# Small extra loads of wo rows from ScalarE and GpSimd in a decode kernel fed by one stream of large loads

## Chip, cores and metric

The kernel runs on one core of one Trainium2 chip. The metric is the device time of one execution in microseconds, taken as the median of several runs. Of the kernel before, three runs are shown: 694.17, 694.26 and 695.5 us, median 694.26 us. A further execution was profiled; its records are what the views below show.

## The reference

One token passes through two blocks whose results are mixed by a gate. Cut to what matters:

```python
q = (x @ wq)                                # 32 heads of 128, x is 1x512
k, v = k_cache, v_cache                     # 8 KV heads x 32768 x 128, each serves 4 query heads
p = softmax(q . k * 128**-0.5)              # over the 32768 keys
a = (p . v) @ wo                            # wo is 4096 x 512
b = (silu(x @ w1) * (x @ w3)) @ w2          # 512 -> 1792 -> 512
g = sigmoid(sum(x * gate_w))
out = g * a + (1 - g) * b
```

Everything is float32. The two caches are 134 MB each, so nearly all the bytes that the kernel reads are keys and values, each of them used once.

## The kernel before

All large loads are issued by SyncE (SP) on one queue, in the order in which the program lists them. A large load brings 128 partitions of up to 64 KB, 8 MB in all, into one of two buffers, `big_a` and `big_b`. First comes wq, then 16 key units (two heads, a quarter of the keys each), w1 and w3 after the fourth key unit, and 16 value units. From the fifth key unit on, keys and values alternate: keys into `big_a`, values into `big_b`. At the end stand four value units with the two halves of wo between them, and then w2 in five pieces of falling size (`parts`, four, four, three, two and one of its 14 row groups), whose last one ends the stream of loads.

The loop over key units, `for t in range(NH)`, has 16 rounds. In each round ScalarE copies three quarters of the second half of the unit away (`set_aside`, L318), VectorE transposes the unit in eight steps (`scores`, L346), TensorE multiplies each transposed piece with the queries (L330), ScalarE copies the scores out (L358), and TensorE works on the value unit of four rounds before (L432). After every fourth round there is a softmax (L379 to L398), and `own` reduces the value result of a head pair into one of six tiles `red` (L448). After the loop, `heads`, `place` and `mix` turn the six tiles into rows, multiply them with the first half of wo, and the last two head pairs follow as their values come in. The last matmuls (L676) use the last pieces of w2, VectorE copies the sum out (L688), and SyncE and ScalarE store two rows of 512 B each (L485).

The order is written out by hand. `Program.add` records every operation with the tiles that it reads and writes and works out which semaphores it must wait for; an operation waits for the last writer of what it reads or writes and for the readers of what it overwrites. Each engine then issues its own operations strictly in order, so an operation that waits holds up everything behind it on the same engine. The scores and values of the loop run from a loop on TensorE (L703 to L735).

GpSimd sets constants at the start (L213 to L223) and then does nothing until the end, where it waits for the two stores (`wait_ge(pr.semaphore("stored"), 32)`). ScalarE issues two small loads at the start (x and gate_w, L202, one row of 2 KB each) and one of the two stores at the end.

Of the kernel before, what the change touches and what calls it, by code (L numbers as in the profile page):

```python
# [13 lines left out]
P = 128  # L14
# [102 lines left out]
def kernel(  # L117
# [13 lines left out]
    nc = tc.nc  # L131
# [23 lines left out]
    pr = Program(nc, tc.alloc_semaphore)  # L155
    pe, dve, act, pool = (
        lambda fn, _e=e, **kw: pr.add(_e, fn, **kw) for e in ("PE", "DVE", "ACT", "POOL")
    )
    V, A, T = nc.vector, nc.scalar, nc.tensor

    def sbuf(name, *shape):
        return nc.alloc_sbuf_tensor(name, [P, *shape], F32)[:]
# [13 lines left out]
    rows = [probs[:, 0, 512 * i:512 * i + 512] for i in range(2)]  # L176
    tmp = sbuf("tmp", 2, 4, P)
    silu, prod = (tmp[:, i].rearrange("p b d -> p (b d)") for i in range(2))
    red = [sbuf(f"red{h}", P) for h in range(6)]
    acc = sbuf("acc", 512)  # L180
    otp = sbuf("otp", 16, 32)
    htp = sbuf("htp", FR, 32)
# [7 lines left out]
    def load(dst, src, writes, over=()):  # L190
        lanes[0] += 1
        lane = f"load{lanes[0] % 9}"
        return pr.add(
            "SP", lambda: nc.sync.dma_start(dst, src), writes=writes, over=[*over, lane], inc=lane, by=16, also=lane,  # L194
        )
# [13 lines left out]
    gate, sums, recip, on = sbuf("gate", 2), sbuf("sums", 32), sbuf("recip", 32), sbuf("on", 32)  # L209
    mt, mtt, mark, mark2 = sbuf("mt", 32), sbuf("mtt", 32), sbuf("mark", 1), sbuf("mark2", 1)  # L210
    quads, high, wide_t, top = sbuf("quads", 4), sbuf("high", 1), sbuf("wide_t", 32), sbuf("top", 32)
    G = nc.gpsimd
# [12 lines left out]
    for src, dst, view, axes in (  # L225
# [11 lines left out]
            reads=[src], writes=[dst])  # L237
# [6 lines left out]
    def clear(**kw):  # L244
        pe(zeros,
           reads=["acc"], writes=["s"], **kw)
# [15 lines left out]
    for c in range(NC):  # L262
# [19 lines left out]
        reads=["gate0"], writes=["gate1"])  # L282
# [4 lines left out]
    for b in range(2):  # L287
        qt = kt[b][:, 0:512]
        dve(lambda b=b, qt=qt: V.transpose(qt, rows[b]), reads=[f"row{b}"], writes=[f"kt{b}"])
        for j in range(4):  # L290
            w, u = divmod(4 * b + j, 2)
            src = qt[32 * j:32 * j + 32, :].rearrange("p (q c x) -> p x c q", q=4, c=4)[:, 0]
            for e in range(2):
                r, o = 2 * u + e, 16 + 8 * e + 4 * u
                dst = win[32 * r:32 * r + 32, w, :, o:o + 4]
# [8 lines left out]
    def where(t):  # L304
        return 1 if t in (0, 2) else 0

    def load_keys(t):
        b = where(t)
        load(big[b], kd[t // 4, t % 4], ["AB"[b] + str(z) for z in range(2)])
# [6 lines left out]
    def set_aside(t):  # L316
        src, key = region(where(t), 1).rearrange("p (n r) -> p n r", n=NB), "AB"[where(t)] + "1"
        act(lambda: A.copy(spare, src[:, :, 32:128]), reads=[key], writes=["wo"])  # L318
        if t == LAG - 1:
            act(lambda: A.copy(extra, src[:, :, 0:32]), reads=[key], writes=["extra"], over=["B1"])  # L320

    def window(t, z):
        return act(
            lambda: A.copy(winc, win[:, t // 4, :, 16 - 16 * z:48 - 16 * z]),  # L324
            reads=[("win", t // 4, r) for r in range(4)], writes=["winc"], credit="windows",
        )
# [9 lines left out]
    def scores(t, z, win_op):  # L336
        kin = region(where(t), z).rearrange("p (n c j) -> p c n j", c=4, j=32)
        ks = []
        for c in range(4):
            src, key = kin[:, c], "AB"[where(t)] + str(z)  # L340
            if (z, c) >= (1, 1):
                src, key = spare[:, :, 32 * (c - 1):32 * (c - 1) + 32], "wo"
            elif z == 1 and t == LAG - 1:
                src, key = extra, "extra"
            dst = kt[c % 2].rearrange("p (n i) -> p n i", i=32)
            k = dve(lambda d=dst, s=src: V.transpose(d, s), reads=[key], writes=[f"kt{c % 2}"], credit="keys")  # L346
            pe(lambda c=c: scores_part(c), reads=[f"kt{c % 2}", "winc"], writes=["s"], loop=True,
               credits=((win_op, 1), (k, 1)) if c == 0 else ((k, 1),))
            ks.append(k)

        if t == LAG - 1 and z == 0:
            done = dve(lambda: V.tensor_copy(mark2, ones[:, 0:1]), reads=["ones"], writes=["mark2"])
            for k in ks:
                k.via = done

    def scores_out(t):
        o = act(
            lambda: A.copy(sb[:, :, :, t % 4], ps_s.rearrange("p (n i) -> p n i", i=32)),  # L358
            reads=["s"], writes=[("sb", t % 4)], credit="scores",
        )  # L360
        return o
# [9 lines left out]
    def turn(loop, credits=()):  # L371
        for f in range(4):
            pe(lambda f=f: turn_part(f), reads=[("sb", m) for m in range(4)] + ["ident"], writes=[f"f{f}"], loop=loop,
               credits=credits if f == 0 else ())
# [29 lines left out]
    def total(w):  # L404
        dve(lambda: V.tensor_reduce(  # L405
            sums[:, 8 * w:8 * w + 8].rearrange("p (u q) -> p u q", u=2),
            probs[:, :, 0:1024].rearrange("p u (n q) -> p u q n", q=4), axis=AX.X, op=ALU.add,
        ), reads=[("prob", u) for u in range(2)], writes=[("sums", w)])


    def load_values(s):
        return pr.add(
            "SP", lambda: nc.sync.dma_start(big[1], vd[s // 2, s % 2]), writes=["B0", "B1"], over=["extra"],
            credit="values", by=16,
        )

    def weights(s):
        u, e = s // 2 % 2, s % 2
        return act(
            lambda: A.copy(  # L420
                pv[:, 0:512].rearrange("p (y r) -> p y r", r=64),
                prob[u][:, 0:1024].rearrange("p (y e r) -> p y e r", e=2, r=64)[:, :, e],
            ), reads=["pvpad", ("prob", u)], writes=["pv"], over=["o"], credit="weights",
        )
# [13 lines left out]
    def values_loop(vt, wt, credits):  # L438
        pe(values_all, reads=["B0", "B1", "pv", "pvpad"], writes=["o"], credits=(*credits, (vt, 16), (wt, 1)), loop=True)


    def own(s):
        h, e = divmod(s, 2)
        dve(lambda: V.tensor_tensor(
            tmp[:, e], ps_o.rearrange("p (b d) -> p b d", b=4), own_b.unsqueeze(2).to_broadcast([P, 4, P]), op=ALU.mult,
        ), reads=["o", "own_b"], writes=[f"tmp{e}"])
        if e == 1:
            dve(lambda: V.tensor_reduce(red[h], tmp.rearrange("p e b d -> p d (e b)"), axis=AX.X, op=ALU.add),  # L448
                reads=["tmp0", "tmp1"], writes=[("red", h)])


    def load_hidden():
        for z, t in enumerate((w1, w3)):
            load(big[1][:, z * NC * F:(z + 1) * NC * F], t.rearrange("(p c) f -> p (c f)", c=NC), [f"B{z}"])

    def hidden_products():
        for z in range(2):
            def ff(z=z):
                t = big[1][:, z * NC * F:(z + 1) * NC * F]
                for c in range(NC):  # L460
                    for j in range(4):
                        o = c * F + FJ * j
                        ins = T.matmul(
                            pm[z][32 * j:32 * j + 32, 0:FJ], xp[:, c, :], t[:, o:o + FJ],
                            start=(c == 0), stop=(c == NC - 1),
                        )
                return ins
            pe(ff, reads=[f"B{z}", "xp"], writes=[f"m{z}"])
# [14 lines left out]
    def store(e, src, key, inc):  # L483
        i, q = (0, nc.scalar) if e == "ACT" else (1, nc.sync)
        pr.add(e, lambda: q.dma_start(outs[2 * i:2 * i + 2, :], src[31 + 64 * i:33 + 64 * i, :]),  # L485
               reads=[key], writes=[("out", i)], inc=inc, by=16)

    load_keys(0)
    vals = {}
    first = window(0, 0)  # L490
    for t in range(NH):
        v = t - LAG
        set_aside(t)
        scores(t, 0, first)
        scores(t, 1, window(t, 1))
        out_op = ((scores_out(t), 1),)
        if v < 0:
            clear(loop=True, credits=out_op)
        if t == LAG - 1:
            load_hidden()  # L500
        if t + 1 < NH:
            load_keys(t + 1)
            first = window(t + 1, 0)
        if v >= 1:
            own(v - 1)
        if t % 4 == 3:
            turn(v >= 0, out_op if v >= 0 else ())
        if v >= 0:
            values_loop(vals.pop(v), weights(v), () if t % 4 == 3 else out_op)
            clear(loop=True)  # L510
        if t == LAG - 1:
            hidden_products()
        if v + 1 >= 0 and t + 1 < NH:
            vals[v + 1] = load_values(v + 1)

        if t % 4 == 3:
            softmax(t // 4)
        if t % 4 == 0 and t > 0:
            total(t // 4 - 1)
        if t == LAG:  # L520
            hidden()
    total(NP - 1)


    own_rows = sbuf("own_rows", 16)
    each = [sbuf(f"each{i}", 16, 8 * n) for i, n in enumerate((2, 1))]


    def load_wo(j, dst, key, over=()):
# [167 lines left out]
    a, b, c, d = flips  # L697
# [33 lines left out]
        values_all().then_inc(done, 1)  # L731
        zeros().then_inc(done, 1)
    pr.emit("PE", ops[d:])
    nc.gpsimd.wait_ge(pr.semaphore("stored"), 32)
    critical.close()  # L735


# [26 lines left out]
```

## Time and profile before

| what | value |
|---|---|
| median of three runs | 694.26 us |
| the profiled execution's own time | 694.09 us |
| its span (first to last instruction) | 692.3 us |
| busy TensorE (matmul) / VectorE / ScalarE / GpSimd | 56% / 53% / 19% / 0% of the span |
| moved by the 16 DMA engines | 296.35 MB, mean 428 GB/s |
| ScalarE instructions / GpSimd instructions counted | 113 / 15 |

The span is 1.8 us shorter than the execution's own time; what lies around the span is not in any view. The page's strip of 40 slices gives the busy share of each engine in tenths; its line "DMA" is the mean busy share of the core's 16 DMA engines. In the views by window, a DMA packet is counted in full in the window in which it starts, so a short window can show more than 1.00. Semaphore and branch instructions, and the issue of DMAs, are not counted as busy.

### The profile page before, as it was taken

How to read it: one execution, taken by the hardware profiler on the slowest of the kernel's cores; microseconds unless marked ns; L12 is line 12 of the kernel's file. 1: busy time of each engine (PE TensorE's matmuls, PEld its weight loads, DVE VectorE, ACT ScalarE, POOL GpSimd, SP SyncE). 2: the span in 40 equal slices, each digit the busy share in tenths (PEclk: the TensorE clock that was granted, in tenths of full speed). 3: DMA queues.
4: the chain of work that ended last, by engine and by line, in shares of the span. 5: the costliest groups of instructions: out<-in, count | busy, mean ns of one | idle time of the engine just before them, and what ended most of it. 6: DMA issues, size and time to landing. Idle time of an engine off the chain costs nothing. (4 is left out here: it accounts for less than half of the span.)

```text
span 692.3 us, 5789 instructions
## 1 busy us (share of the span) xinstructions
PE 386.8 (56%) x2448; PEld 96.5 (14%) x2448; DVE 369.9 (53%) x259; ACT 134.7 (19%) x113; POOL 2.8 (0%) x15
## 2 busy tenths in 40 slices
PE   1437777566463646555473735475563726674467
PEld 0101111201010101101010101101010102221112
DVE  1049998393725637493826537492816546710701
ACT  0143223232303131220303131220303031100000
POOL 1000000000000000000000000000000000000000
PEclk9969999878696877778687879867696966766689
DMA  9999999999999999999999999999999999999996
GB/s 379 467 424 424 428 424 432 456 432 428 428 428 432 439 451 428 428 424 432 432 462 428 424 428 428 432 447 443 428 424 428 428 439 458 400 449 425 426 427 285
DMA packets 6213, 296.35 MB, mean 428 GB/s; under 512 B 694, under 2 KB 698, under 8 KB 1084
## 3 DMA queue, kind: packets, MB, share of 16 engines
q1 hardware_dynamic: 6196, 296.23, 99.1%
q8 instruction: 6, 0.10, 0.1%
q14 instruction: 3, 0.02, 0.0%
q10 hardware_dynamic: 8, 0.01, 0.0%
HBM read 296.23 MB, written 0.00 MB: 428 GB/s over the span
## 5 line engine op out<-in xcount | busy, mean ns | idle before, releaser
L346 DVE STREAM_TRANSPOSE aside<-big_a 128x2048 f32<-128x2048 f32 x41 | 94.3, 2300 | 185.5 <-DMA big_a<-in_A_k_cache_dram 185.5
L330 PE MATMUL ps<-aside,winc 128*32 128x512 f32 x512 | 88.5, 768 | 171.6 <-PEq L703 170.7
L330 PE MATMUL ps<-kt,winc 128*32 128x512 f32 x512 | 88.4, 768 | 50.5 <-PEq L703 50.5
L318 ACT COPY aside<-big_a 128x6144 f32<-128x6144 f32 x14 | 74.4, 5312 | 171.1 <-DMA big_a<-in_A_k_cache_dram 171.1
L432 PE MATMUL ps<-big_b,pv 128*32 128x512 f32 x768 | 92.7, 638 | 17.6 <-PEq L703 17.6
L346 DVE STREAM_TRANSPOSE kt<-aside 128x2048 f32<-128x2048 f32 x32 | 72.7, 2272 | 0.0
L346 DVE STREAM_TRANSPOSE kt<-big_a 128x2048 f32<-128x2048 f32 x28 | 63.6, 2270 | 0.0
L330 PEld LDWEIGHTS ps<-aside,winc 128*32 128x32 f32 x512 | 13.0, 119 | 238.9 <-issue 238.9
L358 ACT COPY sb<-ps 128x512 f32<-128x512 f32 x16 | 17.1, 1070 | 137.6 <-PE ps L330 137.6
L432 PEld LDWEIGHTS ps<-big_b,pv 128*32 128x32 f32 x768 | 27.6, 117 | 83.7 <-issue 83.7
L346 DVE STREAM_TRANSPOSE aside<-aside 128x2048 f32<-128x2048 f32 x16 | 36.3, 2269 | 0.0
L330 PEld LDWEIGHTS ps<-kt,winc 128*32 128x32 f32 x512 | 12.9, 119 | 126.0 <-issue 126.0
L587 PE MATMUL ps<-big_b,probs 128*32 128x512 f32 x128 | 18.3, 729 | 17.4 <-DMA big_b<-in_A_v_cache_dram 17.4
L596 DVE TENSOR_SCALAR red<-ps,own_b 128x128 f32<-128x128 f32 x2 | 0.7, 350 | 49.8 <-PE ps L587 49.8
L324 ACT COPY winc<-win 128x128 f32<-128x128 f32 x32 | 9.8, 308 | 77.7 <-PE ps L330 77.7
L587 PE MATMUL ps<-big_a,probs 128*32 128x512 f32 x128 | 19.5, 778 | 8.0 <-DMA big_a<-in_A_v_cache_dram 8.0
L346 DVE STREAM_TRANSPOSE aside<-big_b 128x2048 f32<-128x2048 f32 x7 | 16.0, 2292 | 11.6 <-DMA big_b<-in_A_k_cache_dram 11.6
L641 PE MATMUL ps<-win,ones 128*128 128x512 f32 (+1 forms) x40 | 21.7, 628 | 0.0
L242 PE MATMUL ps<-acc 128*128 128x512 f32 x34 | 20.0, 670 | 2.4 <-POOL acc L213 1.5
L379 DVE TENSOR_REDUCE mt<-turned 128x8 f32<-128x2048 f32 x4 | 9.2, 2292 | 22.7 <-PE turned L368 22.7
L405 DVE TENSOR_REDUCE sums<-probs 128x8 f32<-128x2048 f32 x4 | 15.3, 3829 | 2.1 <-ACT probs L398 2.1
L268 PE MATMUL turned<-big_a,xp 128*32 128x512 f32 x64 | 8.3, 680 | 11.7 <-DMA big_a<-in_A_wq_dram 11.7
(94 smaller groups left out, 190.6 us busy)
## 6 DMA issues: line engine op xcount, KB each, us to landing
big_b<-in_A_v_cache_dram SPq DMA_DIRECT2D x2, 4096.0 KB, 26.2
big_b<-in_B_w_dram SPq DMA_DIRECT2D x2, 3584.0 KB, 20.8
aside<-in_A_wo_dram SPq DMA_DIRECT2D x1, 4096.0 KB, 28.5
big_a<-in_A_wo_dram SPq DMA_DIRECT2D x1, 4096.0 KB, 19.1
big_a<-in_B_w_dram SPq DMA_DIRECT2D x2, 1024.0 KB, 22.3
big_a<-in_B_w_dram SPq DMA_DIRECT2D x1, 768.0 KB, 24.6
big_a<-in_B_w_dram SPq DMA_DIRECT2D x1, 512.0 KB, 25.4
big_a<-in_B_w_dram SPq DMA_DIRECT2D x1, 256.0 KB, 25.6
```

What stands on the lines that cost most here:

```text
L242: return T.matmul(ps_s, acc[:, 0:P], acc, start=True, stop=False, skip_group_check=True)
L268: ins = T.matmul(pf[b][32 * j:32 * j + 32, :], xp[:, c, :], t[:, o:o + REP * DH], start=(c == 0), stop=(c == NC - 1),)
L318: act(lambda: A.copy(spare, src[:, :, 32:128]), reads=[key], writes=["wo"])
L324: lambda: A.copy(winc, win[:, t // 4, :, 16 - 16 * z:48 - 16 * z]),
L330: ins = T.matmul(ps_s[32 * g:32 * g + 32, :], winc[:, c, :], kt[c % 2][:, 512 * g:512 * g + 512], start=False, stop=False, skip_group_chec ...
L346: k = dve(lambda d=dst, s=src: V.transpose(d, s), reads=[key], writes=[f"kt{c % 2}"], credit="keys")
L358: lambda: A.copy(sb[:, :, :, t % 4], ps_s.rearrange("p (n i) -> p n i", i=32)),
L379: dve(lambda: V.tensor_reduce(mt[:, 0:8], turned.rearrange("p (n q) -> p q n", q=8), axis=AX.X, op=ALU.max), reads=banks, writes=["mt"])
L405: dve(lambda: V.tensor_reduce(sums[:, 8 * w:8 * w + 8].rearrange("p (u q) -> p u q", u=2), probs[:, :, 0:1024].rearrange("p u (n q) -> p u ...
L432: ins = T.matmul(ps_o[32 * t:32 * t + 32, :], pv[:, o:o + 32], big[1][:, n * P:(n + 4) * P], start=((z, g) == (0, 0)), stop=((z, g) == (1, ...
L587: ins = T.matmul(ps_o[32 * t:32 * t + 32, :], prob[u][:, o:o + 32], vt[:, n * P:(n + 4) * P], start=((e, z, g) == (0, 0, 0)), stop=((e, z, ...
L641: return T.matmul(bank[:, 0:n], ones, win.rearrange("p w c n -> p (w c n)")[:, 0:n], start=True, stop=True)
```

## The change

Three things are edited.

1. `rows_early(t)` is called at the end of each round of the key loop, after the softmax and `total` of that round and ahead of `hidden`. In rounds 0 to 8 ScalarE issues small loads of the first n rows of wo, 2 KB each, into partitions 0 to n-1 of the tiles `red[2]` to `red[5]`, which hold nothing at that time: n is 2, 3, 4 and 5 in rounds 0 to 3, and then two loads a round, (6, 7), (8, 9), (10, 11), (12, 13), (14, 15). These are 14 loads with 119 rows. Each one writes the same tiles as the one before it, so it waits until that one has landed. Nothing reads these rows: `own` overwrites the tiles later, and waits for the last of these loads before it first does.
2. In rounds 4, 6, 8, 10 and 12 GpSimd issues loads of 4, 4, 8, 6 and 1 rows, of each row two pieces of 512 B, into partitions 0 to n-1 of the tile `each[0]`, 23 rows in all. Each waits for the one before and for an operation of VectorE. `place` overwrites the tile after the loop, and waits for the last of them. These rows are not read either.
3. GpSimd's wait for the stores gets an increment of the semaphore, which keeps it from being folded into the branch behind it: it becomes an instruction of its own.

Besides, the six tiles `red` become slices of one tensor, and `own_rows` and `each` are declared earlier. SyncE's list of loads is the same, as are TensorE's instructions; VectorE has the same instructions and two more waits.

```diff
-    red = [sbuf(f"red{h}", P) for h in range(6)]
+    reds = sbuf("reds", 6, P)
+    red = [reds[:, h] for h in range(6)]
...
+    own_rows = sbuf("own_rows", 16)
+    each = [sbuf(f"each{i}", 16, 8 * n) for i, n in enumerate((2, 1))]
+    free = reds[:, 2:6].rearrange("p h d -> p (h d)")
+    few = {t: ks for t, ks in enumerate(((2,), (3,), (4,), (5,), (6, 7), (8, 9), (10, 11), (12, 13), (14, 15)))}
+
+    def rows_early(t):
+        for n in few.get(t, ()):
+            pr.add("ACT", lambda n=n: nc.scalar.dma_start(free[0:n, :], wo[0:n, :]),
+                   writes=[("red", h) for h in range(2, 6)], inc="few", by=16)
+        n, key = {4: (4, ("sums", 0)), 6: (4, ("red", 0)), 8: (8, ("red", 1)), 10: (6, ("red", 2)), 12: (1, ("red", 3))}.get(t, (0, 0))
+        if n:
+            src = wo[0:n, :].rearrange("p (a b) -> p a b", a=2)[:, :, 0:P]
+            dst = each[0][0:n].rearrange("p k t -> p (k t)").rearrange("p (a b) -> p a b", a=2)
+            pool(lambda: G.dma_start(dst, src), reads=[key], writes=["each0"], inc="soft", by=16)
...
         if t % 4 == 0 and t > 0:
             total(t // 4 - 1)
+        rows_early(t)
         if t == LAG:
             hidden()
     total(NP - 1)
...
-    own_rows = sbuf("own_rows", 16)
-    each = [sbuf(f"each{i}", 16, 8 * n) for i, n in enumerate((2, 1))]
...
-    nc.gpsimd.wait_ge(pr.semaphore("stored"), 32)
+    landed = pr.semaphore("stored")
+    nc.gpsimd.wait_ge(landed, 32).then_inc(landed, 1)
```

## The prediction

> **What bounds the kernel now.** I read the page's first lines, then the DMA queues, the chain of waits, and last the windows around the end.
>
> ```profile
> span 692.3 us, 5789 instructions
> PE 386.8 (56%) x2448; PEld 96.5 (14%) x2448; DVE 369.9 (53%) x259; ACT 134.7 (19%) x113; POOL 2.8 (0%) x15
> DMA  9999999999999999999999999999999999999996
> ...
> q1 hardware_dynamic: 6196, 296.23, 99.1%
> q8 instruction: 6, 0.10, 0.1%
> q14 instruction: 3, 0.02, 0.0%
> q10 hardware_dynamic: 8, 0.01, 0.0%
> ```
>
> No compute engine is busy for 60% of the span, while SP's queue q1 keeps 16 DMA engines busy for 99.1% of it. I call each of the 16 a lane. ScalarE's queue, q10, has 8 packets in all; q8 and q14 fetch code.
>
> The windows tell how fast the stream is and how it ends. Last columns: DMA share and GB/s.
>
> ```profile
> 22.00:100.00 78.00, 48.36 (x276) 10.84 (x277) 54.51 (x27) 23.86 (x30) 0.00 (x0) 0.91 1.00 434
> 100.00:500.00 400.00, 222.78 (x1408) 51.83 (x1408) 236.37 (x145) 91.41 (x67) 0.00 (x0) 0.80 1.00 434
> ```
>
> ```profile
> 685.00:686.00 1.00, 0.84 (x12) 0.16 (x8) 0.00 (x0) 0.00 (x0) 0.00 (x0) 1.00 1.05 424
> 686.00:687.00 1.00, 0.43 (x4) 0.00 (x0) 0.50 (x1) 0.00 (x0) 0.00 (x0) 1.00 0.74 289
> 687.00:687.50 0.50, 0.28 (x12) 0.28 (x16) 0.18 (x1) 0.00 (x0) 0.00 (x0) 1.00 0.39 156
> 687.50:688.00 0.50, 0.50 (x28) 0.50 (x20) 0.00 (x0) 0.00 (x0) 0.00 (x0) 1.00 0.37 143
> 688.00:688.50 0.50, 0.36 (x16) 0.09 (x12) 0.00 (x0) 0.00 (x0) 0.00 (x0) 1.00 0.18 70
> 688.50:689.00 0.50, 0.50 (x16) 0.32 (x16) 0.00 (x0) 0.00 (x0) 0.00 (x0) 1.00 0.00 0
> ```
>
> 434 GB/s over 16 lanes is 27.1 GB/s each, with the same figure in both long windows. At the end the lanes don't stop together. From 687 to 688 the share is 0.39 and 0.37, so six lanes of 16 still work while ten are done; the last of the six stop at about 688.5. Of the 0.74 between 686 and 687 the six make 0.375; the other 0.365 x 16 = 5.8 lane-us belong to the ten, 0.58 us each, so an early lane ends at 686.6 on average, **2.0 us before the last one**. Each load gives every lane the same number of packets, so nothing evens this out. That nine code fetches (q8 and q14) are to blame for the six late lanes is a guess.
>
> The chain of waits says what hangs on the last lane (start, us, what):
>
> ```profile
> 663.01 25.39 DMA big_a<-in_B_w_dram
> ...
> 688.45 1.10 PE turned L676 x24
> ...
> 689.57 0.29 DVE winc L688
> ```
>
> The last piece of w2, its matmuls, one copy, the stores. So a microsecond on the lane that ends last is a microsecond of time; a microsecond on an early lane costs nothing until its 2.0 us are used up.
>
> **The change, part by part.** Nothing is removed. Added are 119 + 23 rows on the lanes, 19 issues with their waits, two waits on VectorE, one instruction at the end.
>
> *The price of one row.* Three rows of small packets:
>
> ```profile
> q10 hardware_dynamic: 1, 0.00, 1.1%
> ```
>
> ```profile
> DMA packets 22, 0.03 MB, mean 70 GB/s; under 512 B 5, under 2 KB 5, under 8 KB 22
> ...
> q1 hardware_dynamic: 22, 0.03, 18.4%
> ```
>
> ```profile
> q10 hardware_dynamic: 4, 0.00, 10.1%
> ```
>
> The first is the window 7.5 to 8, with the gate_w row in the midst of the stream: 1.1% of 16 x 0.5 us is 88 ns for 2 KB. The second is 688.0 to 688.5, w2's last piece: 18.4% of 8 us is 1.47 us for 17 rows of 2 KB and 5 completions, at most 87 ns a row. The third is ScalarE's store in a window of 45 ns (690.645 to 690.69): 10.1% of 0.72 us is 73 ns of packets within 45 ns, so its two rows ran on two lanes at once. I take it that n rows go to n lanes, one each. At 27.1 GB/s 2 KB alone are 75.6 ns and 1 KB 37.8 ns.
>
> *Who pays?* The trace of before has no small load of several partitions, and 27.1 GB/s may be the pace of the sender (the lane) or of the place that receives. If of the **sender**, a lane gets at most one row of each of the 14 loads: 0 to 14 rows, 0 to 1.2 us. If of the **receiver**, the rows crowd, since all go to partitions 0 to 14, and 16 lanes share 128 partitions, eight each. Partition p is written by the loads with n > p: 14, 14, 13, 12, 11, 10, 9, 8 rows for p = 0 to 7. If a receiver took one of these partitions it would get 14 rows, if all eight, 91. The stream of full packets into that receiver is held up by these rows, whoever sends them. Halfway between 14 and 91 is 53, 53 x 75.6 ns = **4.0 us**. GpSimd's rows go the same way: 5 on partition 0, all 23 on 0 to 7, halfway 14, x 37.8 ns = 0.5 us. Between sender and receiver I take the receiver: the one constant row is 27.1 GB/s for each of 16 equal streams into disjoint eighths, whatever ran beside them, and a receiver that is full explains it as well as a lane does; the crowd onto few partitions is what this change adds that no load before it has.
>
> [...]
>
> *What hides it.* If the loaded stream is an early one (10 in 16), its 2.0 us go first: 4.0 + 0.5 - 2.0 = **2.5 us**. If that cover is gone (6 in 16), nearly all 4.5 us count.
>
> *ScalarE's waits.* A small load is slow to land beside the stream:
>
> ```profile
> L253 PEld LDWEIGHTS ps<-ident,probs x4: 192/213/215, 10.6 to 10.9; 1*128 1x128 f32 x4
> ...
> L202 ACTq DMA_DIRECT2D probs<-in_gate_w_dram x1: 228/228/228, 1.5 to 1.5; - x1
> ```
>
> Issued at 1.5, used at 10.6: 9.1 us. In rounds 4 to 8 the second load waits that long for the first, and ScalarE's next copy queues behind it. Round 7 is the tightest, ScalarE first, then VectorE:
>
> ```profile
> 286.66 1.94 ACT L398 ACTIVATE probs<-turned 128x1024 f32<-128x1024 f32 x2
> 292.90 5.31 ACT L318 COPY aside<-big_a 128x6144 f32<-128x6144 f32 x1 [4.30 <-DMA big_a<-in_A_k_cache_dram]
> ```
>
> ```profile
> 303.97 2.27 DVE L346 STREAM_TRANSPOSE kt<-aside 128x2048 f32<-128x2048 f32 x1
> ```
>
> The exponentials end at 288.6; 9.1 us and two issues of 0.23 later it is 298.2, where L318 began at 292.9. It would end at 303.5, just ahead of the transpose at 303.97 that reads it. Nothing is lost, and if a microsecond were, this holds the stream:
>
> ```profile
> big_a<-in_A_k_cache_dram SPq DMA_DIRECT2D x14, 26.3
> ```
>
> 26.3 us from issue to landing, of which 8.39 MB at 434 GB/s are 19.3: SP issues about 7 us before the last lane is through, some 4 us before the first lane needs it (less the lateness and the start). A lane that starved would be an early one. In the other rounds ScalarE has nothing due for longer. The first wait of VectorE falls in round 10, two rounds after the last load of ScalarE, the other after the loop: nothing.
>
> *GpSimd.* Nothing is queued behind its loads but the last wait. An instruction of its own there is on the path: not below 0, and at most like the smallest instruction that POOL shows:
>
> ```profile
> L223 POOL MEMSET pv<- 128x16 f32 x1 | 0.1, 113 | 0.0
> ```
>
> I take 0.05 us.
>
> *Sum* against the profiled execution's own 694.09: 4.0 + 0.5 - 2.0 + 0.05 = 2.6 (rounded), so **696.7 us**. The median of the runs, 694.26, is 0.17 above that execution, which I leave within the range.
>
> **The rivals.**
>
> A. *Only the sender pays* (not slower by what can be told). Then the six late lanes get between 0 and 14 rows, 7.4 on average; the unluckiest about 10 x 84 ns = 0.84, GpSimd's some 2 x 56 = 0.11, and 0.05: 695.1. For it: the gate_w row cost hardly more in the stream (88 ns) than the rows of the last piece in the calm (87). Against it: that was one row, sent to one partition. It decides as soon as a receiver has room beside 27.1 GB/s.
>
> B. *The rows fall on early lanes or into gaps*: 0.05 us, 694.1. Against it: 14 loads, six late lanes.
>
> C. *Faster.* [...] If the stream gained 0.3%, two of 686 us, 692.1. Against it: keys alone (22 to 100) and keys mixed with values (100 to 500), differently laid out, both run at 434 GB/s. [...]
>
> D. *The crowded stream is a late one already*, the 4.5 us count in full: 694.09 + 4.5 + 0.05 = 698.7.
>
> **How the numbers follow.** Forecast 0.48, A 0.24, B 0.06, C 0.12, D 0.10. The likeliest gives 696.7. The range goes from B, 694.1, to D with a little over, 698.9; it leaves out C and what lies above. A measurement here tells about 0.2%, 1.4 us, from no change. Slower than that: forecast and D, 0.58. Within: A and B, 0.30. Faster: C, 0.12.
>
> **What would show it.** If the receiver pays: the windows of the last microseconds show one or two lanes (shares of 0.06 to 0.13) at work for about 2.5 us after the others, the last w2 landing at about 691, while the long windows stay at 434 GB/s until the very end. If only the sender pays, the six lanes stay together and end within 1 us of 688.5. If C, the windows of 100 to 500 show over 434. ScalarE's L318 of round 8 should begin some 5 us late, and VectorE's transposes not. The prediction is wrong if the end of the last load has not moved though the rows are there, or if the time came from a gap in the stream or from behind the last load.

## The result and the profile after

The changed kernel takes **698.1 us** (median of three runs, 698.01 to 698.66), the kernel before 694.26 us. The ratio is 1.0056, with a 95% interval of 1.0043 to 1.007: slower by 3.84 us. The profiled execution of the changed kernel took 698.01 us, its span 696.2 us; against the profiled one of before (694.09 and 692.3) that is 3.9 us more in both.

The page's lines after, span and DMA queues:

```profile
span 696.2 us, 5814 instructions
...
q1 hardware_dynamic: 6196, 296.23, 98.8%
q10 hardware_dynamic: 246, 0.25, 0.1%
q8 instruction: 5, 0.08, 0.0%
q0 software_dynamic: 160, 0.02, 0.0%
```

SP's queue moves the same 296.23 MB in the same 6196 packets. q10 has the 119 rows of ScalarE with their completions; q0 is new and holds GpSimd's rows. Together they are 0.27 MB, about 0.6 us at 434 GB/s, so the bytes alone explain little of the 3.84 us.

Where the time lies is read from the last steps of the chain of waits (start, us, what):

```profile
666.41 25.56 DMA big_a<-in_B_w_dram
691.97 0.04 issue
692.02 1.08 PE turned L690 x24
693.09 0.02 issue
693.12 0.29 DVE winc L702
```

In the kernel before, the piece of w2 that this chain waits for came at 688.40 (663.01 + 25.39); here it comes at 691.97. These are **3.57 us of the 3.9**, all ahead of the last matmuls. What follows differs by 0.36 us. The last stores, before and after:

```profile
689.89 0.33 SPq L485 DMA_DIRECT2D out_dram<-winc  x1
```

```profile
693.43 0.33 SPq L486 DMA_DIRECT2D out_dram<-winc  x1
```

From there to the end of the span it is 692.3 - 689.89 = 2.41 us before and 696.2 - 693.43 = 2.77 us after.

The windows of the changed kernel's end (next to last column: DMA share):

```profile
688.00:689.00 1.00, 0.61 (x10) 0.01 (x2) 0.00 (x0) 0.00 (x0) 0.00 (x0) 1.00 0.95 377
689.00:690.00 1.00, 1.00 (x8) 0.15 (x8) 0.00 (x0) 0.00 (x0) 0.00 (x0) 1.00 0.63 248
690.00:691.00 1.00, 0.24 (x12) 0.18 (x12) 0.69 (x1) 0.00 (x0) 0.00 (x0) 1.00 0.27 109
691.00:691.50 0.50, 0.50 (x25) 0.50 (x21) 0.00 (x0) 0.00 (x0) 0.00 (x0) 1.00 0.16 61
691.50:692.00 0.50, 0.40 (x16) 0.13 (x7) 0.00 (x0) 0.00 (x0) 0.00 (x0) 1.00 0.06 25
692.00:692.50 0.50, 0.48 (x16) 0.38 (x16) 0.00 (x0) 0.00 (x0) 0.00 (x0) 1.00 0.01 4
```

Before, six lanes went on after the ten others and stopped nearly together. Here the lanes stop one after the other over 3 us: 0.27 of 16 is four lanes, 0.16 between two and three, and 0.06 is **one lane that works alone for the last half microsecond**. The stream as a whole has lost something too: from 100 to 500 it runs at 432 GB/s where it ran at 434, which over 400 us is some 1.8 us (an estimate: each of the two rates is rounded to 1 GB/s). A gain, the sign of rival C, is not to be seen:

```profile
100.00:500.00 400.00, 220.32 (x1400) 50.16 (x1400) 232.84 (x143) 91.13 (x66) 3.05 (x5) 0.79 1.00 432
```

### The profile page after: what moved, and what is told of

It reads as the page before. It is cut to its first block, busy times and chain, and to the rows that moved or that the text cites. A ratio compares the mean times of both kernels' runs of the same rounds, so it can differ in the third digit from the quotient of the medians.

```text
span 696.2 us, 5814 instructions
## 1 busy us (share of the span) xinstructions
PE 384.2 (55%) x2448; PEld 94.7 (14%) x2448; DVE 369.9 (53%) x259; ACT 134.7 (19%) x113; POOL 5.9 (1%) x20
## 3 DMA queue, kind: packets, MB, share of 16 engines
q1 hardware_dynamic: 6196, 296.23, 98.8%
## 5 line engine op out<-in xcount | busy, mean ns | idle before, releaser
L331 PE MATMUL ps<-kt,winc 128*32 128x512 f32 x512 | 85.8, 746 | 51.3 <-PEq L717 51.3
L433 PE MATMUL ps<-big_b,pv 128*32 128x512 f32 x768 | 95.1, 652 | 17.5 <-PEq L717 17.5
L601 PE MATMUL ps<-big_a,probs 128*32 128x512 f32 x128 | 17.9, 722 | 8.2 <-DMA big_a<-in_A_v_cache_dram 8.2
L269 PE MATMUL turned<-big_a,xp 128*32 128x512 f32 x64 | 9.9, 785 | 11.9 <-DMA big_a<-in_A_wq_dram 11.9
```

The source lines that it names most:

```text
L269: ins = T.matmul(pf[b][32 * j:32 * j + 32, :], xp[:, c, :], t[:, o:o + REP * DH], start=(c == 0), stop=(c == NC - 1),)
L331: ins = T.matmul(ps_s[32 * g:32 * g + 32, :], winc[:, c, :], kt[c % 2][:, 512 * g:512 * g + 512], start=False, stop=False, skip_group_chec ...
L433: ins = T.matmul(ps_o[32 * t:32 * t + 32, :], pv[:, o:o + 32], big[1][:, n * P:(n + 4) * P], start=((z, g) == (0, 0)), stop=((z, g) == (1, ...
L601: ins = T.matmul(ps_o[32 * t:32 * t + 32, :], prob[u][:, o:o + 32], vt[:, n * P:(n + 4) * P], start=((e, z, g) == (0, 0, 0)), stop=((e, z, ...
```

## The experiments

**The theories.** Receiver: rows that go to neighbouring partitions meet in one place, hold up the stream of large packets into it and wait in line themselves. Costly row: a row costs its own lane some 0.25 us (3.57 / 14), wherever it goes. GpSimd: its loads do the harm. Each kernel ran on the same chip as runs of the kernel before, whose median was 694.20 us beside the first four of the table, 694.13 beside the next three and 694.12 beside the last three. The last loads' arrival and the stretch from the stores to the end are read as above, from the one profiled execution of each kernel; the arrivals of kernels that took as long as the one before differ by up to 0.5 us (688.24 to 688.71). The ratio is the recorded one; it can differ by 0.0003 from that of the two medians.

| run | median us | ratio to before, 95% | last piece of w2 arrives | stores to end |
|---|---|---|---|---|
| ScalarE's rows only | 696.83 | 1.0036 (1.0023 to 1.005) | 690.91 | 2.39 |
| GpSimd's rows only | 694.76 | 1.0008 (0.9999 to 1.0017) | 688.44 | 2.76 |
| ScalarE's rows, four partitions apart | 695.92 | 1.0022 (1.0013 to 1.0032) | 690.34 | 2.47 |
| one GpSimd load | 694.40 | 1.0001 (0.9992 to 1.001) | 688.24 | 2.50 |
| four rows in one group | 696.64 | 1.004 (1.0026 to 1.0054) | 690.67 | 2.38 |
| four rows in four groups | 695.41 | 1.0018 (1.0009 to 1.0027) | 689.64 | 2.47 |
| rows from partition 64 | 697.85 | 1.0055 (1.0041 to 1.0069) | 691.51 | 2.40 |
| the wait alone | 694.10 | 0.9998 (0.9989 to 1.0007) | 688.65 | 2.37 |
| one row | 694.14 | 0.9999 (0.999 to 1.0008) | 688.31 | 2.41 |
| two rows | 694.18 | 1.0001 (0.9992 to 1.001) | 688.71 | 2.42 |

### Which engine's rows

ScalarE's rows only:

```diff
-        n, key = {4: (4, ("sums", 0)), 6: ...
-        if n:
-            ...
-            pool(lambda: G.dma_start(dst, src), ...)
...
-    landed = pr.semaphore("stored")
-    nc.gpsimd.wait_ge(landed, 32).then_inc(landed, 1)
+    nc.gpsimd.wait_ge(pr.semaphore("stored"), 32)
```

> ScalarE's 14 loads stay, GpSimd's five loads and the changed wait are taken out. Receiver theory (rows hold up the stream into the partitions they are written to): the last load is through 2.9 to 3.6 us later than before (GpSimd's rows are worth at most 17 x 0.038 = 0.65 of the 3.57 seen), and the stretch from the stores to the end is that of before again (2.4 us instead of 2.8), so about 697.2 us. Theory of the costly row (each row costs its own lane about 3.57 / 14 = 0.25 us wherever it is written): the same here. GpSimd theory (its loads do the harm): 694.3 us, as before.

Measured 696.83 us, 2.63 more than before. The chain of this run:

```profile
664.41 26.50 DMA big_a<-in_B_w_dram
690.91 0.04 issue
690.96 1.10 PE turned L685 x24
```

The last piece comes at 690.91, 2.51 us later than before and a little less than expected. ScalarE's rows alone do most of it.

GpSimd's rows only:

```diff
-    few = {t: ks for t, ks in enumerate(((2,), (3,), ...
+    few = {}
```

> GpSimd's five loads and the wait of its own stay, ScalarE's 14 loads are taken out. Receiver theory: 0.65 us on a stream that, if an early one, has 2.0 us to spare, so the last load is not later, and only the 0.36 us behind the stores are left: 694.6 us. Costly row: 3 rows at most on a lane, at most 0.4 us more: 694.6 to 695.0. GpSimd theory: some 3.9 us more, 698 us.

Measured 694.76. The chain:

```profile
662.07 26.37 DMA big_a<-in_B_w_dram
688.44 0.04 issue
688.49 1.11 PE turned L690 x24
```

688.44 against 688.40: alone, GpSimd's rows are hidden, and only the longer stretch behind the stores is left. The GpSimd theory falls. But the same rows are not free beside ScalarE's: with both the last piece comes at 691.97, without GpSimd's at 690.91, **1.06 us** for what cost nothing alone (0.85 us by the medians: 3.84 - 2.63 - 0.36). That fits a cover of 2.0 us that can be spent once.

### Where the rows go

Row i to partition 4 i:

```diff
-            pr.add("ACT", lambda n=n: nc.scalar.dma_start(free[0:n, :], wo[0:n, :]),
+            pr.add("ACT", lambda n=n: nc.scalar.dma_start(free[0:4 * n:4, :], wo[0:n, :]),
```

> As the run with ScalarE's rows only, but row i of each load is written to partition 4 i instead of partition i: the same loads, bytes and lanes, other receivers. Receiver theory: the rows of a load meet in fours on the first partitions no more; what is left is up to 14 rows x 88 ns on a lane and a few foreign rows, so the last load is 0.5 to 1.6 us later than before: 694.8 to 695.9 us. Costly row: the same as with the rows side by side, about 697.2 us.

Measured 695.92: the same rows cost 1.72 us instead of 2.63. The costly row alone doesn't forecast that. The expectation's upper end was 695.9, and the two intervals overlap (1.0023 to 1.005 and 1.0013 to 1.0032), so two sharper kernels followed, both with 14 loads of four rows each at the same places and none by GpSimd. The second has the step of four partitions above as well.

```diff
-    few = {t: ks for t, ks in enumerate(((2,), (3,), ...
+    few = {t: (4,) * k for t, k in enumerate((1, 1, 1, 1, 2, 2, 2, 2, 2))}
```

> ScalarE issues 14 loads of four rows each, to partitions 0 to 3, at the same places; no GpSimd load, the wait as before. 56 rows in all, fewer than half of the 119. Receiver theory: all 56 go into one stream, 56 x 0.0756 = 4.2 us, less 2.0 if that stream is an early one, and the four senders stand in line with them: the last load 2.2 to 4.2 us later, 696.4 to 698.4 us. Costly row (a row costs its own lane alone): 14 rows on four lanes; with 88 ns a row 694.2 to 695.4 us.

> The same 14 loads of four rows, written to partitions 0, 4, 8 and 12. Receiver theory, with groups of four partitions: no two rows of a load meet, each lane pays 14 x 88 ns = 1.2 us, hidden on an early lane: 694.2 to 695.4 us, and no big packet is stretched while the rows come in. Costly row: the same time as with partitions 0 to 3.

Side by side in partitions 0 to 3 they cost 2.51 us (696.64), at 0, 4, 8 and 12 they cost 1.28 us (695.41), and while the two intervals just touch, the runs are apart: the fastest of the first took 696.33 us, the slowest of the second 695.57. Same loads, bytes, number and places in the program; only the partitions differ. The costly row falls.

The packets show what happens to the large loads meanwhile. Below are packets, MB and share of SP's queue from 310 to 330, when ScalarE's last two loads run; first the kernel before, then the four rows in four groups, the four rows in one group, the rows four partitions apart, ScalarE's rows side by side, and the changed kernel:

```profile
q1 hardware_dynamic: 162, 8.98, 103.7%
```

```profile
q1 hardware_dynamic: 158, 8.85, 102.2%
```

```profile
q1 hardware_dynamic: 152, 8.65, 100.2%
```

```profile
q1 hardware_dynamic: 147, 8.52, 99.5%
```

```profile
q1 hardware_dynamic: 144, 8.39, 99.1%
```

```profile
q1 hardware_dynamic: 144, 8.39, 99.6%
```

All large packets here are of 64 KB, so 8.98 MB are 137 of them and the other 25 are completions, of 0.009 us each. The share times 16 x 20 us, less the completions, by the number of large packets is the mean time of one: (331.8 - 0.2) / 137 = **2.42 us** before. By the same working 326.8 / 135 = **2.42** with four rows in four groups, 320.5 / 132 = **2.43** with four rows in one group, 318.3 / 130 = **2.45** with the rows apart, 317.0 / 128 = **2.48** side by side, 318.6 / 128 = **2.49** in the changed kernel (the rounding of the share is worth 0.001). Four rows that meet no other row leave the large packets alone, and pay only their own time.

For the pair that differs in the partitions alone these means are nearly the same, and the single packet records of the two traces show why. With four rows in one group, one packet for each of the two loads takes 2.67 us (they start at 318.49 and 326.08), and all the others of the window take 2.42 to 2.44. With four groups none takes over 2.43. The difference, 0.25 us, is three rows of 84 ns, which is what a record of one row shows. I read this as one lane, the one that writes where the four rows meet, waiting for the three that other lanes send. It is not every packet that is stretched.

With 14 and 15 rows side by side many packets are: 37 of the 128 take over 2.45 us, and all of them together lose 128 x 0.056 = 7.2 us of lane time to the 29 rows of that window, 0.25 us a row.

The rows apart still stretch the packets a little (2.45 us against 2.42), where the four rows at 0, 4, 8 and 12 do not (2.42). In the packet records of the rows apart the loads of 9 and 10 rows lengthen the large packets by only 0.06 and 0.15 us in all, that of 11 rows by 0.6, and those of 12 to 15 rows by 1.6 to 3.3 us. Whether that comes from the partitions that the later rows of a load go to, or from that many rows at once, wherever they go, no run separates. That partitions go by fours was the author's assumption; no other step was run.

Rows from partition 64 on:

```diff
-            pr.add("ACT", lambda n=n: nc.scalar.dma_start(free[0:n, :], wo[0:n, :]),
+            pr.add("ACT", lambda n=n: nc.scalar.dma_start(free[64:64 + n, :], wo[0:n, :]),
```

> As the run with ScalarE's rows only (14 loads of 2 to 15 rows side by side), but written from partition 64 on instead of 0. Receiver theory: the rows crowd in the same way, on other streams: 2 to 3.5 us more than before, 696.2 to 697.7 us; the size depends on whether the streams that are hit are late ones. If the harm were tied to partitions 0 to 14 or to the lanes that send alone, it would be small here (under 695) or the same as with partitions 0 to 14 (696.8).

Measured 697.85, 3.72 us more, a little over the range. Nothing hangs on partitions 0 to 14; from 64 on the crowd cost more, 3.72 us against 2.63. Why it is 1 us worse there no run tried. In the packet records, strung into lanes as told under "The cover" below, the large packets of two lanes are stretched by 3.9 and 3.0 us in all, those of the others by 1.3 to 2.0, and the second of the two, which ends last, is a late lane. So a late stream is hit there; that this makes the whole 1 us was not shown.

### Who has cover

Four rows in four groups cost 1.28 us, 14 rows x 88 ns = 1.23 for a lane without cover. So one of these four lanes had to be a late one. One row (partition 0) and two rows (0 and 4) test the other half, that an early lane hides them.

```diff
-    few = {t: (4,) * k for t, k in enumerate((1, 1, 1, 1, 2, 2, 2, 2, 2))}
+    few = {t: (1,) * k for t, k in enumerate((1, 1, 1, 1, 2, 2, 2, 2, 2))}
```

and `(2,) * k` for two rows, both with the step of four.

> 14 loads of one row each by ScalarE, to partition 0, so 14 x 88 ns = 1.2 us on one lane. With four rows in four groups the time rose by 1.28 us, so one of those four lanes is a late one. If this lane is an early one, its 2.0 us hide the rows: 694.1 to 694.3 us; if it is the late one, 695.4 us.

> 14 loads of two rows each, to partitions 0 and 4. With both lanes early: 694.1 to 694.3 us; with a late one among them 695.0 to 695.4 us. Nothing between, if a lane either has 2.0 us to spare or next to none.

Measured 694.14 and 694.18 against 694.12: **nothing** that can be told, and the intervals, which end at 1.0008 and 1.001, leave out 1.2 us (0.0017). The 14 loads have the same issues and waits on ScalarE. The first two lanes are early, the third or the fourth is late. The packet records of the four groups agree: the lane that ends last there sends 14 rows and holds two code fetches.

### Behind the stores

One GpSimd load, and the wait alone (in this order, each a change to another kernel: the changed one with `few = {}` as above, and the one before):

```diff
-        n, key = {4: (4, ("sums", 0)), 6: (4, ("red", 0)), 8: (8, ("red", 1)), 10: (6, ("red", 2)), 12: (1, ("red", 3))}.get(t, (0, 0))
+        n, key = {12: (1, ("red", 3))}.get(t, (0, 0))
...
-    landed = pr.semaphore("stored")
-    nc.gpsimd.wait_ge(landed, 32).then_inc(landed, 1)
+    nc.gpsimd.wait_ge(pr.semaphore("stored"), 32)
```

> Of all added loads only GpSimd's last one, of one row, is left, and the wait is folded into the branch as before. If the 0.36 us behind the stores come from GpSimd having issued any load at all, the stretch from the stores to the end is 2.7 to 2.9 us and the time 694.6 us; if they come from the wait being an instruction of its own, it is 2.4 us and the time 694.3 us. The end of the last load should stay where it was before in all theories.

```diff
-    nc.gpsimd.wait_ge(pr.semaphore("stored"), 32)
+    landed = pr.semaphore("stored")
+    nc.gpsimd.wait_ge(landed, 32).then_inc(landed, 1)
```

> The kernel before with nothing but GpSimd's last wait as an instruction of its own. If the wait costs what the stretch from the stores to the end grew by in the changed kernel, that stretch is 2.8 us and the time 694.5; if GpSimd's five loads made that stretch longer, it is 2.4 us and the time 694.1, as before.

The wait as an instruction of its own, alone: 694.10, the stretch 2.37. It costs nothing. One GpSimd load, wait folded: 2.50, between the two cases of the expectation and hardly above the 2.37 to 2.47 of the runs without a GpSimd load (a span is given to 0.1 us). GpSimd's five loads, alone or with ScalarE's: 2.76 and 2.77. So it is the loads of GpSimd that lengthen the stretch, by some 0.35 us for five of them, long after they have landed. The instruction records of the traces show in which instruction it sits: the first DRAIN of GpSimd behind its wait takes 41 ns in the kernel before and with the wait alone, 125 ns after one load, and 474 ns after five, in both kernels that have them.

## Why the prediction was right, and where its sizes were off

**Bound and direction.** The stream of loads is the bound, the lane that ends last sets the end, and the added rows delayed it, by 3.57 us: as predicted. The end of w2 was forecast at about 691 and came at 691.97; 698.1 us lies within the range. The signs came only in part. One or two lanes were to work alone for about 2.5 us, but there were four of them until 691 and a single one only for the last half microsecond; and the stream was to stay at 434 GB/s, but ran at 432. The rows cost every lane something and the last one most, where the prediction counted one stream. The packets of the last lane follow one another with no gap over 0.2 us, so the time did not come from a gap in the stream; 0.36 us of it came from behind the last load.

**The row's price.** 88 ns on its own lane: confirmed by the four rows in four groups (1.28 us against 1.23), when the lane is a late one. In this the sender of rival A pays as well. A alone was too small: with the four rows in one group it is twice as much (2.51 against 1.28).

**Who pays.** "Between sender and receiver I take the receiver" was the right choice, but both pay. The packet records, strung into lanes as under "The cover", show how. With four rows in one group the lane that ends last is an early one. Its own large packets are stretched by 2.7 us in all (their time over 2.42 us each, from 60 to 335 us), and it sends 14 rows besides, 14 x 84 ns = 1.2 us. The three other lanes that send 14 rows have 0.0 to 0.7 us of stretch, the most where code is fetched too. In the changed kernel the last lane is again an early one with 14 rows, and its stretch is 3.6 us. So the path was that of the forecast: a crowded stream that was early, less its cover. The size was off. The prediction had 53 rows into one stream, 4.0 us, less 2.0 of cover; ScalarE's rows alone measured 2.51 by the chain, 2.63 by the medians: the term was 0.5 to 0.6 too small. It took 75.6 ns a row where its own rows showed 84 to 88; at 84 ns the 53 rows are 4.45 us, and 2.45 is left (an estimate). No run shows that 53 rows meet in one stream; what the runs show is 2.51 us for 56 rows in partitions 0 to 3 and 2.63 us for 119 rows in partitions 0 to 14. That it came so near is in part luck: 53 stood as the middle between 14 and 91, and it left out that in the run with ScalarE's rows only every lane has at least 0.7 us of stretch, even one that sends a single row.

**The cover.** 2.0 us on an early lane: one and two rows vanish, 1.2 us on a lane, and so do GpSimd's rows alone; its full size was not tried by a run. The guess on the code fetches is borne out by the trace of before, though no run tried it. The packet records name no engine, but a packet starts some 4 ns before the one ahead of it on its lane has ended, so they can be strung into 16 lanes, and each lane then has the same 387 packets of SP's loads. Ten lanes end at 686.2 to 687.2 and six at 688.1 to 688.6. Five of the six hold one fetch of 16 KB, of 0.9 to 1.07 us, and the sixth two of 8 KB, of 0.33 us each. Of the ten only one holds any, of 0.31 us. (One of the nine fetches comes after the stream, at 691.24.) In the other traces too I call a lane late when it holds such fetches.

**GpSimd's rows.** Forecast 0.5, measured 1.06 beside ScalarE's by the chains and 0.85 by the medians. The 23 rows meet each other and the crowd's last lane; that this doubles them was only argued, and the cause stays open.

**The end.** Forecast 0.05 for the wait, with "Nothing is queued behind its loads but the last wait". The wait costs nothing, and the loads cost 0.36 us behind the stores, which no row of before could show. (The MEMSET that gave the bound, 113 ns, was not POOL's smallest: those of L750 take 100 to 103.) In sum: 2.0 became 2.5, 0.5 became 1.1, 0.05 became 0.36; 2.6 became 3.9.

**ScalarE's waits.** This step failed in its size and was right in its effect. Round 7 of the changed kernel, ScalarE:

```profile
286.83 1.94 ACT L399 ACTIVATE probs<-turned 128x1024 f32<-128x1024 f32 x2
294.35 0.31 ACTq L496 DMA_DIRECT2D reds<-in_A_wo_dram  x1
295.11 5.31 ACT L319 COPY aside<-big_a 128x6144 f32<-128x6144 f32 x1 [6.34 <-DMA big_a<-in_A_k_cache_dram]
```

The second load goes out at 294.35, some 5.6 us after the exponentials, not 9.1 us and an issue. L318 of round 8 was to begin some 5 us late and began 2.2 us late. The copy at 295.11 waits for the keys, which come 2.2 us later than before (292.90) with the late lanes, and not for ScalarE. VectorE's transposes, which were not to move, shift with the keys, and SP issues the next keys at 307.52, 2.2 us later than before; the stream goes on at 432 GB/s all the same.

**The rivals.** B falls with the time, C with the windows (432 GB/s, not over 434); no run shows the gain of 0.3% that it took. D, a crowded stream that was late from the start, forecast 698.7 and is nearer in size, but the last lane of the changed kernel holds no code fetch, so by the packet records it was an early one.

## What to carry to other kernels

Here one stream of loads set the time, and its end was the end of the slowest DMA engine: 691.97 us, when the first to stop had been done for some 3 us. In such a kernel read the last microseconds in short windows, see how many engines still work, and ask of every added transfer on which engine and into which partitions it falls. 14 loads of four rows in neighbouring partitions cost the saturated stream 2.51 us, where their 0.11 MB at 434 GB/s are 0.26 us (an estimate); with each row four partitions from the next they cost 1.28 us, about their own time on a lane (14 x 88 ns = 1.23), and one or two rows, on lanes with cover, nothing that can be told (694.14 and 694.18 us against 694.12). With up to 15 rows a load the distance helped, but did not make them free of each other (1.72 us instead of 2.63). Cover was spent once: GpSimd's rows, free alone (688.44 against 688.40 us), cost 1.06 us beside ScalarE's.

## What the runs showed of the hardware beyond that

A transfer of 0.27 MB beside a stream of 296 MB, 0.09% of the bytes, made the kernel 0.56% slower. GpSimd loads that had landed more than 200 us earlier lengthened the last stretch of the kernel by 0.35 us (five loads; 2.76 against 2.41). Rows of the same size cost 3.72 us from partition 64 on and 2.63 us from partition 0 on.
